# A recurrence and a SwiGLU block on one core: the transposed k made by VectorE and DRAM, the state's matmuls put beside the following unit's scores, sums merged, the beginning in another order

## The chip, the cores and the metric

The kernel runs on one core of a Trainium2 chip. The metric is the time of one execution on the device in microseconds (us), as the median of several runs. The profile is that of one further execution, with times from the start of its span. All arithmetic is in 32-bit floats; the weights arrive as 64-bit words and are made into 32-bit floats on the chip.

## The reference

The input is `q`, `k`, `v` and `f_logit`, each 4 batches x 8 heads x 768 positions x 48, and three weight matrices. A gated linear recurrence runs over the positions of each batch and head, and its output, laid out as 3072 tokens of 384, goes through a SwiGLU block of 1536 hidden values:

```python
f = 1.0 / (1.0 + np.exp(-f_logit))
for t in range(S):
    state = f[:, :, t, :, None] * state + np.einsum('bhd,bhe->bhde', k[:, :, t], v[:, :, t])
    y[:, :, t] = np.einsum('bhd,bhde->bhe', q[:, :, t], state)
x = y.transpose(0, 2, 1, 3).reshape(B * S, H * D)
g = x @ w_gate
out = (g * (1 / (1 + np.exp(-g))) * (x @ w_val)) @ w_out
```

## The kernel before

**Units.** The 768 positions are cut into 6 chunks of 128. A unit is one batch and one chunk (all 8 heads), so there are 24, taken chunk by chunk, with b = 0 to 3 in each. `short_path` does the work; `general_path` follows only if the smallest product of gates in a chunk, which `judge` looks at near the end, is below 2^-60, and in these runs it is not.

**One unit's attention** is the generator `attention(u)` (from line 518); each `yield` ends a step, and the caller decides when the next one is traced. Keys, queries and gates are held transposed, as 48 rows of one head under 48 rows of another in each of four blocks of 128 positions. ScalarE makes the sigmoid (L532, or L535 in the first two chunks). From chunk 2 on (`SQUARES`), the input is loaded as 32x32 squares that VectorE's stream transpose turns (L538 for the gates, L545 for `kT`, L565 for `qT`); before that TensorE transposes it. A scan on VectorE (L549) gives `tails`, the products of the gates to the chunk's end; its first column, `whole`, is the decay of the whole chunk. `kT` is multiplied by it (L559), which is the decayed k. A second scan gives `head` (L562), by which `qT` is multiplied (L568). `decayed` is the state times `whole` (L572).

TensorE then makes the scores `sc` from `kT` and `qT` (L586, 8 matmuls, which are 16 records in the profile), and transposes `kT` into the bank `kt` (L590, 4 records), which ScalarE copies to SBUF (L594). VectorE multiplies the scores by the causal mask into `A` (L596, twice). The output `y` is `decayed` times `qT` plus `v` times `A`: for b < 3 in two banks with 64 columns of weights a time (L614, L618), then two copies on ScalarE and 10 small DMAs from SP's queue into `xT`; for b = 3 with 32 columns a time, from a `diagonal` form of `decayed` that ScalarE copies (L578), straight into the layout of `xT` (L639, copy L654). The state's increment `dS` is `kt` times `v` (L659, 16 records of 48 columns), and VectorE adds it to `decayed` (L666). In the last chunk `kt` and `dS` are left out.

**The feed-forward block.** Chunk 0 uses plain matmuls (`mlp_plain`: `gate` and `val` at L712, down at L737), while the weights still come in; a weight is fetched, its sizes are taken by two ScalarE operations (`sizes`) and joined by VectorE (`joins`). From chunk 1 on `mlp_fifteen` multiplies the two 384 x 384 block matrices with 15 products in place of 18 (L887), for each of four values of j. A product is two matmuls of 256 columns, four records in the profile, into one of the banks A, B and o; ScalarE copies most of them to SBUF (L892, into `c11`, `c12`, `c22`, `c31`, `c32` or `aside`), VectorE adds and subtracts them (L786, L789), ScalarE takes the silu (L903) and VectorE multiplies gate by value (L837) into the hidden tiles `h`. The 15 products of one j are called a triple here. The token sums `xs` (L847 to L862) and the hidden sums `hs` (L978 to L981) are VectorE's. The down matmul, `down_seven`, uses 7 products in place of 8 (L990, and L1054 for the last, `seven`), whose results VectorE adds into `ob`. Its outputs leave by DMA from ScalarE's queue (`put_out`, L999).

**The order.** The attention of chunk c + 1 is woven into the feed-forward block of chunk c. From chunk 1 on the order is written out by hand: a counter `now` grows by `PRODUCT` (0.86) for a product and by half of `DOWN` (3.9) for half of a down product, and a step of a unit is traced when `now` passes its time in the list:

```python
    STEPS = (-2.6, -1.3, 0, 1.3, 2.8, 3.5)
    UNITS_2 = [[at + t for t in STEPS] + [*rest] for at, rest in (
        (2.6, (4, 9, 12, 14, 17.3, 17.3, 19)), (12.5, (18.2, 24, 28, 30, 34.5, 34.5, 36)),
        (28.5, (35, 41, 51.4, 52.5, 57, 57, 58)), (52, (57.1, 64, 68, 70, 72.5, 72.5, 74)))]
```

The six times from `STEPS` are those of the sigmoid and the VectorE steps up to `kT`, the seven that follow those of `head`, the transpose of q, `qT`, `sc`, `A`, `y` with `dS`, and the state. `lag` puts a VectorE operation one piece later than the product that it uses. `in_order` (L684, called at L1157 and L1219) then holds TensorE, VectorE and ScalarE to the traced order from the first unit to the middle of chunk 0's block, and again from chunk 1's block on; SP's queue is not among the three. Between the two calls `take_turns` alternates the pieces and a scheduler orders them.

**The beginning.** `run(b, step)` (L1106) works through chunk 0's units, whose attention has nothing beside it but fetching weights. Then come four joins of weights and the first steps of chunk 1's unit 4, up to L1157.

**The state's room.** All units share one `decayed` (L374). The four hidden rows of a unit are six tiles `h[j]` (L702), so each sum on them is made six times with 256 columns.

## Time and profile before

| | |
|---|---|
| median of 7 runs | 620.75 us (620.26 to 622.13) |
| profiled execution, its own time | 620.9 us |
| its span | 619.2 us |
| busy: TensorE, VectorE, ScalarE | 599.9, 500.3, 293.7 us |
| chunk 0's units alone | 0 to 31.3 us |
| chunk 0's block, with chunk 1's attention | 31.3 to 149.3 us |
| blocks of chunks 1, 2, 3, 4, with the attention of the next chunk | 94.6, 97.0, 97.1, 93.5 us |
| block of chunk 5, alone, down to its last half product | 76.7 us |
| last half product and last stores | 11.0 us |
| VectorE: stream transpose of 128x512 (L545) | 1123 ns |
| VectorE: sum of 128x256 on hidden tiles (L789) | 421 ns |
| ScalarE: copy of `kt`, 128x512 (L594) | 586 ns |
| ScalarE: table load | 1283 ns |
| store of one output tile, 192 KB, issue to landing | 2.0 us |
| loads of 96 KB squares, issue to landing | 2.3 to 2.4 us |

In the profile a row of a group has the line, the engine, the operation and its operands, the number of instructions, the total busy time, the mean in ns of one, and after the second bar the idle time of the engine just before them with what ended it. In a row in order of time the first number is the start, the second the length, and square brackets hold the idle time before it and its releaser. PE is TensorE's matmuls, PEld its weight loads, DVE VectorE, ACT ScalarE, POOL GpSimd; SPq and ACTq are DMA issues in the queues of SP and ScalarE. A matmul's length overlaps that of the next, so lengths of TensorE rows are not additive; starts are.

### The profile page before, as it was taken

The numbers are of one execution on the slowest core, as the hardware profiler recorded it, in microseconds if no ns is written. First come the engines' busy times: TensorE is split into PE (matmuls) and PEld (weight loads), VectorE is DVE, ScalarE is ACT, GpSimd is POOL, SyncE is SP. The second block draws the span as 40 slices with busy tenths as digits, with TensorE's granted clock in tenths as the row PEclk, the third lists the DMA queues.
The fourth block names the chain that finished last, engine by engine and source line by source line (L and its number), as shares of the span: only waits on it lengthen the run. The fifth ranks groups of instructions, "written<-read, shape, count | busy, mean of one in ns | idle before, by whom it ended". The sixth has DMA issues, their size and how long they took to land.

```text
span 619.2 us, 10913 instructions
## 1 busy us (share of the span) xinstructions
PE 599.9 (97%) x4060; PEld 489.5 (79%) x4060; DVE 500.3 (81%) x961; ACT 293.7 (47%) x535; POOL 5.0 (1%) x27
## 2 busy tenths in 40 slices
PE   7898999999999999999999999999999999999995
PEld 4744545667888898888899788899888889888895
DVE  7889999878999978868897877987887984566741
ACT  2485645313875621557711557632367641365600
POOL 1000000000000000000000000000000000000000
PEclk9999999999999999999999999999999999999998
DMA  9999573005231324212224320323331300100001
GB/s 149 240 244 251 172 233 90 5 23 160 63 87 49 79 69 125 67 47 65 52 72 121 91 52 19 83 62 95 110 77 29 79 7 9 51 2 0 1 2 56
DMA packets 95678, 50.95 MB, mean 82 GB/s; under 512 B 56064, under 2 KB 89472, under 8 KB 95616
## 3 DMA queue, kind: packets, MB, share of 16 engines
q1 hardware_dynamic: 92304, 45.64, 30.4%
q10 hardware_dynamic: 3312, 4.52, 2.0%
q8 instruction: 34, 0.56, 0.4%
q14 instruction: 28, 0.23, 0.1%
HBM read 42.47 MB, written 4.72 MB: 76 GB/s over the span
## 4 chain that ended last, share of the span: by engine, by line
PE 81%; DVE 9%; ACT 4%; DMA 3%; issue 2%; SPq 1%; ACTq 0%; DVEq 0%
PE o L990 16%; PE A L887 16%; PE B L887 13%; PE o L887 5%; PE c L887 5%; PE o L737 5%; PE sc L586 4%; PE val L712 4%; PE gate L712 3%; PE y L618 2%; PE kt L590 2%; PE y L614 1%; PE dS L659 1%; DVE head L562 1%; DMA ksquares<-in_k_dram 1%
## 5 line engine op out<-in xcount | busy, mean ns | idle before, releaser
L887 PE MATMUL A<-xs,w_both 128*128 128x256 f32 x240 | 62.5, 383 | 3.5 <-ACT c L892 2.3
L990 PE MATMUL o<-w_out,h 128*128 128x192 f32 x360 | 62.1, 327 | 0.2 <-ACT aside L892 0.2
L990 PEld LDWEIGHTS o<-w_out,h 128*128 128x128 f32 x360 | 58.6, 190 | 0.8 <-ACT aside L892 0.4
L887 PEld LDWEIGHTS A<-xs,w_both 128*128 128x128 f32 x240 | 44.5, 190 | 12.5 <-ACT c L892 3.9
L892 ACT COPY c<-A 128x512 f32<-128x512 f32 x40 | 23.4, 584 | 64.9 <-DVE ob L786 33.9
L786 DVE TENSOR_TENSOR c<-c,aside 128x512 f32<-128x512 f32 x60 | 41.1, 686 | 14.8 <-ACT aside L892 13.8
L892 ACT COPY aside<-A 128x512 f32<-128x512 f32 x60 | 35.0, 583 | 32.8 <-PE A L887 32.8
L789 DVE TENSOR_TENSOR c<-c,aside 128x512 f32<-128x512 f32 x60 | 41.2, 687 | 7.3 <-ACT aside L892 7.3
L837 DVE TENSOR_TENSOR h<-h,c 128x256 f32<-128x256 f32 x100 | 41.4, 422 | 7.0 <-ACT h L903 6.7
L990 PE MATMUL o<-ws,h 128*128 128x192 f32 x240 | 41.7, 328 | 0.0
L887 PE MATMUL B<-xT,extra 128*128 128x256 f32 x160 | 41.4, 381 | 0.0
L887 PE MATMUL c<-xT,w_both 128*128 128x256 f32 x160 | 41.3, 380 | 0.0
L887 PE MATMUL A<-xs,extra 128*128 128x256 f32 x160 | 41.2, 380 | 0.0
L887 PE MATMUL B<-xs,w_both 128*128 128x256 f32 x160 | 41.1, 379 | 0.0
L903 ACT ACTIVATE h<-c 128x256 f32<-128x256 f32 x100 | 39.2, 415 | 3.2 <-DVE c L789 2.0
L892 ACT COPY aside<-B 128x512 f32<-128x512 f32 x60 | 35.0, 583 | 10.7 <-PE B L887 10.1
L990 PEld LDWEIGHTS o<-ws,h 128*128 128x128 f32 x240 | 39.2, 190 | 0.3 <-issue 0.2
L789 DVE TENSOR_TENSOR c<-o,c 128x512 f32<-128x512 f32 x40 | 27.6, 689 | 14.7 <-ACT h L903 9.5
L596 DVE TENSOR_TENSOR A<-sc,causal 128x512 f32<-128x512 f32 x48 | 30.6, 678 | 6.0 <-PE sc L586 6.0
L887 PEld LDWEIGHTS B<-xs,w_both 128*128 128x128 f32 x160 | 30.4, 190 | 4.1
L887 PEld LDWEIGHTS c<-xT,w_both 128*128 128x128 f32 x160 | 30.2, 190 | 4.4 <-DVE c L789 0.2
L887 PEld LDWEIGHTS A<-xs,extra 128*128 128x128 f32 x160 | 30.3, 190 | 4.2
(134 smaller groups left out, 1154.6 us busy)
## 6 DMA issues: line engine op xcount, KB each, us to landing
fsquares<-in_f_logit_dram SPq DMA_DIRECT2D x64, 96.0 KB, 2.3
ksquares<-in_k_dram SPq DMA_DIRECT2D x64, 96.0 KB, 2.3
qsquares<-in_q_dram SPq DMA_DIRECT2D x64, 96.0 KB, 2.4
v<-in_v_dram SPq DMA_DIRECT2D x24, 192.0 KB, 3.1
w<-in_moe_w_gate_dram SPq DMA_DIRECT2D x6, 768.0 KB, 6.2
w<-in_moe_w_val_dram SPq DMA_DIRECT2D x6, 768.0 KB, 5.4
w<-in_moe_w_out_dram SPq DMA_DIRECT2D x6, 768.0 KB, 5.7
out_dram<-ob ACTq DMA_DIRECT2D x23, 192.0 KB, 2.0
```

The costliest lines, as they stand in the source:

```text
L586: nc.tensor.matmul(sc[par][:, a * C:(a + 1) * C], lhsT=kT[r, a, :], rhs=qT[r, a, :], start=True, stop=True)
L590: nc.tensor.transpose(p[:, a * C:(a + 1) * C], kT[:, a, :], ident)
L596: nc.vector.tensor_tensor(A[:, par], sc[par].rearrange("p (a t) -> p a t", t=C), causal.unsqueeze(1).broadcast_to((128, HP, C)), ALU.mult)
L712: nc.tensor.matmul(p, lhsT=w[:, j, i, :], rhs=xT[c][:, i, :], start=(i == 0), stop=(i == KT - 1))
L737: nc.tensor.matmul(p, lhsT=h[n // 2][:, n % 2 * 2 + b // 2, b % 2 * C:(b % 2 + 1) * C], rhs=w_out[:, j, :], start=(n == 0), stop=(n == NF ...
L786: nc.vector.tensor_tensor(dst, a, b, ALU.add)
L789: nc.vector.tensor_tensor(dst, a, b, ALU.subtract)
L837: lagging.append(lambda: f(*args))
L887: nc.tensor.matmul(p[name][:, n, :], lhsT=weights_of[a][:, n, j, :], rhs=tokens[b], start=fresh and n == 0, stop=True, skip_group_check=True)
L892: nc.scalar.copy(t, p[name])
L903: nc.scalar.activation(dst, src[:, 0, :], AF.Silu)
L990: nc.tensor.matmul(p[:, n, :], lhsT=lhsTs[j][:, n * C:(n + 1) * C], rhs=rhs[:, j, :], start=first and j == order[0] and n == 0, stop=j == ...
```

## The change

The parts, in the order of the diff:

- The decayed k in transposed form. For chunks 2 to 4 TensorE no longer transposes `kT`. VectorE's stream transpose turns each 32x32 square into `beside` (in the buffer of `head`), four DMAs from SP's queue write it to a tile `turn` in DRAM in rows of 32 values, and one DMA reads it back as `kt`. Chunks 0 and 1 keep the matmul transposes.
- Loads of the next unit's squares are issued singly, each right after its room is free, and `v`'s after `dS`.
- Two `decayed` tiles are used in turn.
- `dS` of a unit and the state's sum are given the time of the following unit's `sc` (just before it) and of its `A`, where they were given that of the unit's own `y`. The times in the list change: `SCORES` holds the times of `sc`, `BEHIND` those of `A` and `y` after it. From chunk 3 on the third unit starts at 22.9 where it was 28.5.
- The hidden tiles of even and of odd j are one tile each, and the sums on them are made three at a time (768 columns). Two token sums become one of 512 columns.
- The halves of `seven` get a bank each, and their outputs leave from SP's queue.
- The beginning: one join and two `sizes` come earlier, unit 4's sigmoid is made on the raw input (`sigmoid_ahead`), so that after the transpose there is only a copy, the loads of unit 5 come later and together. SP joins the engines that `in_order` holds.

```diff
+    def sigmoid_ahead(u):
+        fr = raw["f"][u % NRAW]
+        nc.scalar.activation(fr, fr, AF.Sigmoid)
+        ahead.add(u)
...
+        flat_decayed = two_decayed[u % len(two_decayed)]
+        decayed = flat_decayed[:, 0:HP * D].rearrange("p (a d) -> p a d", d=D)
...
-            nc.scalar.activation(pairs(gate)[:, :, 1:N1], p, AF.Sigmoid)
+            nc.scalar.activation(pairs(gate)[:, :, 1:N1], p, AF.Copy if u in ahead else AF.Sigmoid)
...
+        if SQUARES <= c < NCH - 1:
+            beside = att.tile([128, n], FP32, tag="head", name="beside", bufs=1)[:, 0:HP * C]
+            beside = beside.rearrange("p (i m) -> p i m", i=NI)
+            nc.vector.transpose(beside.rearrange("p i (a e) -> p a i e", e=Q), kT.rearrange("p a (i e) -> p a i e", e=Q))
+            turn = turn_pool.tile([Q, NI, HP, NI, Q], FP32, tag="turn", name="turn")
+            for r in range(NI):
+                nc.sync.dma_start(out=turn[:, :, :, r, :].rearrange("t i a e -> t (i a) e"),
+                                  in_=beside[Q * r:Q * (r + 1)].rearrange("t i (a e) -> t (i a) e", e=Q))
         yield
...
-        if c < NCH - 1:
+        if c < SQUARES:
             p = bank("kt")
             for a in range(HP):
                 nc.tensor.transpose(p[:, a * C:(a + 1) * C], kT[:, a, :], ident)
         yield
-        if c < NCH - 1:
-            kt = att.tile([128, H, W], FP32, tag="kt", name="kt")
-            nc.scalar.copy(kt, p.rearrange("t (h d) -> t h d", d=W))
+        kt = att.tile([128, HP * C], FP32, tag="kt", name="kt")
+        if c < SQUARES:
+            nc.scalar.copy(kt, p)
+        elif c < NCH - 1:
+            nc.sync.dma_start(out=kt, in_=turn.rearrange("t i a r e -> i t (a r e)"))
...
+        load_v_after(u)
         yield
...
+    def load_v_after(u):
+        if units[u][1] >= SQUARES and u + 2 < len(units):
+            load(u + 2, "v")
...
-    def hidden_tile():
-        return ffn.tile([128, 4, TH], FP32, tag="h", name="h", bufs=NP)
+    def hidden_tile(h, j):
+        if j % 2 not in h:
+            h[j % 2] = ffn.tile([128, NP // 2, 4, TH], FP32, tag="h", name="h", bufs=2)
+        return h[j % 2][:, j // 2]
...
-    UNITS_2 = [[at + t for t in STEPS] + [*rest] for at, rest in (
-        (2.6, (4, 9, 12, 14, 17.3, 17.3, 19)), (12.5, (18.2, 24, 28, 30, 34.5, 34.5, 36)),
-        (28.5, (35, 41, 51.4, 52.5, 57, 57, 58)), (52, (57.1, 64, 68, 70, 72.5, 72.5, 74)))]
-    UNITS = [[at + t for t in STEPS] + [*rest] for at, rest in (
-        (-10, (-6, 1, 6, 8, 10.5, 10.5, 12)), (6.5, (12, 18, 22.5, 24.5, 27, 27, 29)))] + UNITS_2[2:]
+    SCORES = [[12, 28, 51.4, 68], [6, 22.5, 51.4, 68]]
+    UNITS = [[[k + t for t in STEPS] + [*rest] for k, rest in zip(ks, rests)] for ks, rests in (
+        ((2.6, 12.5, 28.5, 52), ((4, 9, 9.1), (18.4, 24, 24.1), (35.6, 41, 41.1), (57.1, 64, 64.1))),
+        ((-10, 6.5, 22.9, 52), ((-6, 1, 1.1), (12.3, 18, 18.1), (30.1, 37, 37.1), (57.1, 64, 64.1))))]
+    BEHIND = ((2, 6.2), (2, 7.5), (1.1, 5.6), (2, 4.5))
+    for n, at in enumerate(SCORES):
+        following = at[1:] + [whole + SCORES[1][0]]
+        for b in range(B):
+            UNITS[n][b] += [at[b], at[b] + BEHIND[b][0], at[b] + BEHIND[b][1], following[b] - 0.01,
+                            following[b] + BEHIND[(b + 1) % B][0] - 0.01]
...
-                for j in order:
-                    lag(minus, h[j][:, 0, :], s1[j], h[j][:, 0, :])
+                for odd in range(2):
+                    lag(minus, h[odd][:, :, 0, :], s1[odd], h[odd][:, :, 0, :])
...
         def seven(n):
-            if n == 0:
-                kept["p"] = bank2("o3", "A")
+            p = bank2("o3", "Ao"[n])[:, n, :]
...
-            lag(put_out, 0, n, nc.sync if n and c == NCH - 1 else nc.scalar)
+            lag(put_out, 0, n, nc.sync)
...
         run(b - 1, 4)
+    joins.pop(0)()
+    sizes.pop(0)()
     run(B - 1, 3)
+    sizes.pop(0)()
     joins.pop(0)()
     run(B - 1, 4)
 
     hidden, last = mlp_plain(0)
     steps = attention_steps(1)
-    for _ in range(2):
-        sizes.pop(0)()
-        joins.pop(0)()
-    load(B + 1, "v")
+    sigmoid_ahead(B)
+    joins.pop(0)()
     for _ in range(2):
         sizes.pop(0)()
     hidden[0]()
@@
     hidden[1]()
     weights()
+    load(B + 1)
     hidden[2]()
     steps.pop(0)()
-    in_order(mark, (mybir.EngineType.PE, mybir.EngineType.DVE, mybir.EngineType.Activation))
+    in_order(mark, (mybir.EngineType.PE, mybir.EngineType.DVE, mybir.EngineType.Activation, mybir.EngineType.SP))
```

In chunk 1 the parts of a unit in `attention_steps` become 3, 5, 3, 3 where they were 3, 5, 2, 3; there the step with `beside` is empty, so this only counts the added `yield`.

## The prediction

> **What bounds the kernel now.** I read the page's busy shares and its 40 slices first, then busy times by stage, then TensorE's instructions in order of time, then the waits.
>
> ```profile
> PE 599.9 (97%) x4060; PEld 489.5 (79%) x4060; DVE 500.3 (81%) x961; ACT 293.7 (47%) x535; POOL 5.0 (1%) x27
> ...
> PE   7898999999999999999999999999999999999995
> ```
>
> The program is one long TensorE stream. Only the first 50 us and the last ten have visible holes. By stage (length, then busy time of PE, PEld, DVE, ACT and POOL, the granted clock, the DMA share, GB/s):
>
> ```profile
> 149.30:243.90 94.60, 94.14 (x698) 83.29 (x697) 87.62 (x164) 50.65 (x95) 0.42 (x1) 1.00 0.33 83
> 243.90:340.90 97.00, 96.13 (x706) 84.89 (x705) 80.42 (x159) 48.97 (x93) 0.42 (x1) 1.00 0.28 73
> 340.90:438.00 97.10, 96.23 (x706) 85.18 (x706) 80.66 (x160) 48.80 (x93) 0.42 (x1) 1.00 0.28 73
> 438.00:531.50 93.50, 92.44 (x625) 80.97 (x625) 73.06 (x145) 44.84 (x87) 0.42 (x1) 1.00 0.17 46
> ```
>
> The last row is the window in which chunk 5's units run, which need no `kt` and no `dS`; TensorE is idle 1 us or less in each. So a TensorE instruction removed here is time removed, less what the order loses. TensorE in order of time, with a `kt` (chunk 4) and without (chunk 5):
>
> ```profile
> 304.52 1.13 PE L887 MATMUL A<-xT,w_both 128*128 128x256 f32 x4
> 305.58 1.16 PE L586 MATMUL sc<-qT,kT 48*128 48x128 f32 x16
> 306.67 0.66 PE L590 MATMUL kt<-idf,kT 128*128 128x128 f32 x4
> 307.16 4.07 PE L990 MATMUL o<-w_out,h 128*128 128x192 f32 x24
> ...
> 444.80 1.16 PE L586 MATMUL sc<-qT,kT 48*128 48x128 f32 x16
> 445.89 1.13 PE L887 MATMUL B<-xs,extra 128*128 128x256 f32 x4
> ```
>
> Durations overlap, so I take start to start: `sc` 1.09 us, `kt` 0.49. A product (four records) takes 0.86; straight after `sc` it takes 0.97, after `kt` 0.86.
>
> The stall that returns at every chunk's start:
>
> ```profile
> 339.21 4.33 ACTq L999 DMA_DIRECT2D out_dram<-ob  x2
> ...
> 343.59 0.59 ACT L892 COPY c<-A 128x512 f32<-128x512 f32 x1 [8.63 <-DVE ob L786]
> ...
> 344.23 1.13 PE L887 MATMUL A<-xs,w_both 128*128 128x256 f32 x4 [0.58 <-ACT c L892]
> ```
>
> ScalarE's queue holds the output of `seven`, which waits for VectorE's `ob`. The copy of the first product, which frees bank A for the fourth, stands behind it. The third product starts at 342.62, the fourth at 344.23: 1.61 us instead of 0.86, and the fourth itself 0.97.
>
> [...]a product lasts 0.96 before `sc` or `y`, and 0.97 after them. [...]here 128x256 takes 422 ns and 128x512 687, thus 157 ns fixed. [...]No run here shows the price of 128-byte writes to DRAM.
>
> **The change part by part.** Signs are of the time.
>
> *`kt` off TensorE, `dS` beside the next scores* (12 units, chunks 2 to 4). Before, a unit with `y` in two banks costs 0.10 into `sc`, 1.09, 0.49, 0.10 into `y`, 0.60, 0.92, `dS` 0.55, 0.11 out: 3.96. After: 0.10 into `dS`; `dS` ahead of `sc` 0.60 (15.52 to 16.13 in chunk 0, where the two already stand so); 1.09; 0.11; 0.10; 0.60; `y` ahead of a product 1.02 (chunk 5); 0.11: 3.73. So -0.23 for nine units. For the three with b = 3, whose `y` runs at 128x32 and has the same cost out either way, -0.49 + 0.11 = -0.38. Sum -3.2. Bounds: -2.0[...], -4.6 if the moved `dS` is free.
>
> *VectorE's share.* 12 transposes at 1.12 us (the row of `kT<-ksquares`) add 13.4 us. Merged sums: each chunk 24 of 0.42 become 8 of 768 columns, 157 + 768 x 1.035 = 0.95: -2.5, over five chunks -12.6; merged token sums -0.8. Net nothing, and TensorE hides it. But merging pays late in each chunk, and the transposes come early. In 155 to 205 VectorE is busy 49.9 of 50 us and two fall there: 0 to +1. I take 0, because the nearest consumer in the order, `y` of unit 8, has 1.1 us to spare and is put one product (0.86) later. ScalarE loses 12 copies of 0.59, which were not on the path.
>
> *The round trip.* Four writes of 512 pieces of 128 B and one read of 2 KB rows. `v` has 1024 pieces of 192 B and lands in 3.1 us. Twice the pieces: 4 us as my estimate[...], then some 2.5 for the read. Four things wait behind it: `dS` has at least 20 us from the transpose (decayed ends at 160.0, next `sc` at 181.0); the next unit's `head`, whose buffer the transpose borrows, has 8.5 us in one case, 9.7 in three, 12 or more elsewhere; what stands behind `kt`'s load on SP's queue (`yT` to `xT`, three to four products later); SP's issues, five more per unit. All fit: 0.
>
> *Output of `seven` to SP's queue.* The chunk-start stall goes: 0.75 + 0.11, at four starts (245.6, 342.6, 439.5, 533.2): -3.4. What is late next: the copy's own chain, 0.2 + 0.59 after the first product, is ready 0.9 us before the fourth. So all of it counts. On SP the two stores wait for `ob` with the next unit's `turn` behind them, 15 us early.
>
> *The third unit's sigmoid.* Its start moves from 25.9 to 20.3 in the list from chunk 3 on, so on ScalarE it now stands between `c31`'s copy and the silu, with both table loads. TensorE's thirteenth product waits for the `aside` copied after them: 0.2 + 0.58 + 1.28 + 0.63 + 1.28 + 0.32 + 0.58 = 4.9 us after the ninth ends. TensorE has three products and `dS` + `sc` in between: 2.6 + 1.8 = 4.4. +0.55 in three windows: +1.6 (bounds 0 and +2). The same chain with one load makes the stall that stays:
>
> ```profile
> 351.99 1.28 ACT L903 ACT_TABLE_LOAD   x1
> ...
> 354.23 0.73 PEld L887 LDWEIGHTS A<-xs,w_both 128*128 128x128 f32 x4 [0.69 <-ACT aside L892]
> ```
>
> `y` moved to a triple's end hides a 0.13 us hitch there in each of three windows: -0.4.
>
> *The beginning.*
>
> ```profile
> 51.01 0.68 DVE L568 TENSOR_TENSOR qT<-qTp,head 128x512 f32<-128x512 f32 x1
> ...
> 51.83 1.16 PE L586 MATMUL sc<-qT,kT 48*128 48x128 f32 x16 [1.83 <-DVE qT L568]
> ```
>
> TensorE runs unbroken from 31.28, then waits here, after two matmuls of `val` (1.72 us) that the changed order puts behind `sc`. So it arrives at 48.1. VectorE: the first join (1.9 us) now fills the 1.25 us it waited at 26.75, delays A by 0.7 (`gate` still starts near 31.3, since its join is done), and brings the four joins' end from 37.5 to 35.6. The early sigmoid saves ScalarE two table loads of 1.28, so the 1.6 us wait for `top` at 42.9 shrinks to some 0.6; 0.5 waits for the next weights. I get `qT` at 49.1 instead of 51.7: TensorE stalls 1.1 with 1.7 us of `val` still ahead, against 1.83 with none. -0.9. If VectorE gains nothing, +1.6; if `qT` is there in time, -2.0.
>
> *The end.* `seven`'s halves get a bank each; 612.18 shows both halves' `ob` added after the last matmul, and both DMAs (612.6, 612.9) landing together at 617.0. Now one add of 0.35 and one DMA remain; the first store of this kind landed after 2.8. From 612.5: 615.7, -1.3 (0 to -1.6).
>
> Two decayed states remove a buffer wait that nothing on TensorE showed: 0.
>
> Sum: -3.2 - 3.4 + 1.6 - 0.4 - 0.9 - 1.3 = -7.6. The profiled execution took 620.9 (span 619.2 and 1.7 around it), 0.15 over the median of 620.75. So a span of 611.6 and a median of 613.1; I say 613.0.
>
> **The rivals.**
> *VectorE or ScalarE becomes the bound.* Stages with VectorE at 100% take the transposes as delay (+1 in 149 to 208, +0.5 in two later windows), the sigmoid's chain costs 2, the beginning loses 1.6 instead of gaining 0.9. For it: VectorE busy 87.62 of 94.60 us in the first of the windows; against: TensorE's slack to `qT` is 3 to 8 us in later windows. -7.6 + 2 + 0.4 + 2.5, and less where only some come: 615.5 to 618.
> *More is gained.* `dS` moved at no cost (-1.4), no sigmoid stall (-1.6), `qT` in time (-1.1): 609.
> *The other side: the round trip is late.* `head` holds VectorE until `turn` has landed, in order, so all of VectorE stands behind it. It begins at 7.3 us of landing (8.5 less the transpose) and costs TensorE once VectorE's slack of 1 to 4 us is used up. To eat 7.6 us in 12 units, the four writes would have to land in some 13 us; six times as long as the 2.3 of a 96 KB load. At 15 us: about 625. Against: the DMA share is 0.17 to 0.33 in these windows.
> *It does nothing:* the transposes do leave the list and the store does change queues, so only cancelling sums could give this.
>
> **How the numbers follow.** As drawn up: 0.62, with its own range 610.5 to 615.5. VectorE or ScalarE takes over: 0.20. More gained: 0.12. Late round trip: 0.05. No effect: 0.01. From 609 to 617.5 leaves out the rival on the other side, and the tails of the two next to it. Faster by over 0.2% (619.5; about what seven runs of 0.3% spread can tell): 0.94; within: 0.01; slower: 0.05.
>
> **What would show it.** Right: `sc` goes straight to a product of 0.97; `dS` to `sc` 0.60; windows of 97 us shrink to about 95; no wait of A for `c` at chunk starts; a new wait for `aside` at the thirteenth product of the second triple; the last `ob` a single add. Wrong: VectorE waiting at `head` for DMA `turn`; TensorE waiting for `kt` by DMA; a longer wait of the fifth unit's `sc`.

## The result, and the profile after

The changed kernel takes 618.62 us in the median of 14 runs (616.32 to 620.51), against 621.93 for the kernel before in 35 runs, those of the prediction's table among them. The ratio is 0.9951, with a 95% interval of 0.9941 to 0.9962. So it is faster, by some 3 us, where 7.6 were forecast, and it lies above the range. The kernel before lies either at 620.0 to 621.2 or near 622, with a mean granted clock of 0.996 to 0.999 in the first group and 0.994 to 0.996 in the second where the series list it, so below ratios are compared and not medians of different series. One ratio is uncertain by 0.10 to 0.23%, that is 0.6 to 1.4 us, and a difference of two ratios by somewhat more. The profiled execution took 618.05 us, its span 616.0.

The page has TensorE at 595.6 us instead of 599.9, and VectorE as busy as it was:

```profile
PE 595.6 (97%) x4012; PEld 484.5 (79%) x4012; DVE 500.4 (81%) x888; ACT 286.6 (47%) x522; POOL 5.0 (1%) x28
```

By stage, cut at the first product of each block, the blocks of chunks 1 and 2 are (length, then busy time of PE, PEld, DVE, ACT, POOL, the granted clock, DMA share, GB/s):

```profile
147.07:243.87 96.80, 94.41 (x674) 82.83 (x672) 89.78 (x152) 49.89 (x92) 0.42 (x1) 1.00 0.42 103
243.87:339.57 95.70, 94.88 (x689) 83.36 (x689) 81.45 (x146) 47.09 (x89) 0.42 (x1) 1.00 0.39 95
```

The first of them has 2.4 us in which TensorE is idle, where the kernel before had 0.5 in the same stretch. The same cuts in both kernels, beside what the terms of the prediction's sum give for each stretch:

| stretch | before | after | change | forecast |
|---|---|---|---|---|
| to the first product of chunk 1's block | 147.48 | 147.07 | -0.4 | -0.9 |
| block of chunk 1 | 96.38 | 96.80 | +0.4 | -1.1 |
| block of chunk 2 | 97.04 | 95.70 | -1.3 | -1.5 |
| block of chunk 3 | 96.92 | 95.70 | -1.2 | -1.5 |
| block of chunk 4 | 93.67 | 94.77 | +1.1 | -0.4 |
| block of chunk 5 to the last matmul | 80.66 | 79.80 | -0.9 | -0.9 |
| last matmul to the end of the span | 7.06 | 6.16 | -0.9 | -1.3 |
| sum | | | -3.2 | -7.6 |

One `dS` (0.60) has moved from the block of chunk 1 into that of chunk 4, since each now waits for the next unit's scores; with that put right the block of chunk 1 is 1.0 us longer than before, and that of chunk 4 is 0.5 longer.

What TensorE waited for in the changed kernel, in total us, times and the longest:

```profile
PE A L929 <- ACT aside L934: 3.4, 7, 1.1
PE fTp L542 <- DMA fraw<-in_f_logit_dram: 2.8, 2, 2.4
...
PE c L929 <- ACT c L934: 2.0, 1, 2.0
```

Before, this view had 2.3 us in four waits of A for `c`, at the chunk starts, 1.3 in five for `aside` and 1.7 for `fraw`. The four waits at the chunk starts are gone. In their place there is more waiting for `aside`, one wait of 2.0 us for `c`, and one of 2.4 us for the fourth unit's `f` in the beginning. The wait of 1.8 us of chunk 1's first unit for `qT` is gone too.

**What came as forecast.** TensorE in order of time where a unit's scores stand now:

```profile
250.01 0.67 PE L690 MATMUL dS<-v,kt 128*64 128x48 f32 x16
250.61 1.16 PE L615 MATMUL sc<-qT,kT 48*128 48x128 f32 x16
251.70 1.13 PE L929 MATMUL B<-xs,extra 128*128 128x256 f32 x4
252.67 1.03 PE L929 MATMUL c<-xT,w_both 128*128 128x256 f32 x4
```

Start to start, `dS` takes 0.60, `sc` 1.09, the product behind it 0.97: the prediction's numbers. At a chunk's start (all engines, the rows between left out) the copy no longer stands behind the store, which is on SP's queue, and the fourth product starts at 342.16, 0.86 after the third:

```profile
340.63 0.59 ACT L934 COPY c<-A 128x512 f32<-128x512 f32 x1 [6.39 <-PE A L929]
...
341.76 0.85 SPq L1037 DMA_DIRECT2D out_dram<-ob  x2
...
342.16 1.03 PE L929 MATMUL A<-xs,w_both 128*128 128x256 f32 x4
```

At the end one add follows the last matmul (the first row), where there were two (the second row, of the kernel before):

```profile
609.87 0.35 DVE L830 TENSOR_TENSOR ob<-c,o 128x192 f32<-128x192 f32 x1 [1.59 <-PE o L1091]
...
612.18 0.62 DVE L786 TENSOR_TENSOR ob<-c,o 128x192 f32<-128x192 f32 x2 [2.29 <-PE o L1054]
```

**What did not: the first window.** All engines around the 2 us wait, rows between left out:

```profile
189.34 0.42 DVE L881 TENSOR_TENSOR h<-h,c 128x256 f32<-128x256 f32 x1
...
189.85 0.59 ACT L934 COPY c<-c 128x512 f32<-128x512 f32 x1 [3.30 <-DVE h L881]
...
190.49 1.13 PE L929 MATMUL c<-xT,w_both 128*128 128x256 f32 x4 [1.98 <-ACT c L934]
```

The twelfth product of the third triple needs bank c, whose copy on ScalarE needs the room that VectorE's multiplication `h` at 189.34 sets free, and that multiplication stands in a VectorE queue that has next to no gap from 157 to 207 us (busy 49.83 of the 50 us; before, 49.76). The 5 us around the wait, in the changed kernel and then in the one before (TensorE's busy time comes first, VectorE's is the third):

```profile
187.00:192.00 5.00, 3.02 (x28) 2.08 (x26) 4.97 (x13) 1.50 (x4) 0.00 (x0) 1.00 0.67 157
...
187.00:192.00 5.00, 5.00 (x63) 4.16 (x62) 5.00 (x9) 2.86 (x7) 0.00 (x0) 1.00 0.08 22
```

Before, the same copy stood at 189.19 and the product at 191.67, because `y` and `dS` of the second unit came ahead of it:

```profile
189.19 0.59 ACT L892 COPY c<-c 128x512 f32<-128x512 f32 x1 [1.49 <-DVE h L837]
...
189.59 0.67 PE L614 MATMUL y<-qT,decayed 48*64 48x128 f32 x16
...
191.67 1.13 PE L887 MATMUL c<-xT,w_both 128*128 128x256 f32 x4
```

Counted from the first product of the block, the copy begins 1.07 us later than before (42.78 instead of 41.71), and TensorE is there for the product 2.75 us earlier (41.44 instead of 44.19).

**The last window.** The third unit's sigmoid, with a table load on either side, stands ahead of the `aside` that the thirteenth product needs, as forecast. In the blocks of chunks 2 and 3 the wait is 0.54 us each (the first row). In the block of chunk 4, whose units have no `dS`, TensorE is there 0.60 earlier and waits 1.14; the second of the loads and what stands behind it:

```profile
273.97 1.13 PE L929 MATMUL A<-xs,w_both 128*128 128x256 f32 x4 [0.54 <-ACT aside L934]
...
463.14 1.28 ACT L945 ACT_TABLE_LOAD   x1
...
464.75 0.57 ACT L934 COPY aside<-A 128x512 f32<-128x512 f32 x1
...
465.38 1.13 PE L929 MATMUL A<-xs,w_both 128*128 128x256 f32 x4 [1.14 <-ACT aside L934]
```

### The profile page after: what moved, and what is told of

It reads as the page before. It is cut to its first block, busy times and chain, and to the rows that moved or that the text cites. A ratio compares the mean times of both kernels' runs of the same rounds, so it can differ in the third digit from the quotient of the medians.

```text
span 616.0 us, 10805 instructions
## 1 busy us (share of the span) xinstructions
PE 595.6 (97%) x4012; PEld 484.5 (79%) x4012; DVE 500.4 (81%) x888; ACT 286.6 (47%) x522; POOL 5.0 (1%) x28
## 3 DMA queue, kind: packets, MB, share of 16 engines
q10 hardware_dynamic: 2016, 2.75, 1.3%
## 4 chain that ended last, share of the span: by engine, by line
PE 82%; DVE 6%; ACT 4%; DMA 3%; issue 1%; SPq 1%; ACTq 0%; DVEq 0%
PE o L1028 20%; PE A L929 14%; PE B L929 10%; PE gate L751 5%; PE val L751 5%; PE o L774 5%; PE o L929 4%; PE c L929 4%; PE o L1091 3%; PE sc L615 3%; PE y L649 2%; PE y L670 2%; PE dS L690 1%; PE y L645 1%; DMA fraw<-in_f_logit_dram 1%
```

## The experiments

Each is an edit of the changed kernel, unless it says otherwise. "Against the changed kernel" is the difference of the two ratios to the kernel before, times 621 us. Windows of the traces are compared where they say more than a ratio. Some profiles have stretches of 3.41 us, or two or three times that, in which the granted clock is 0.50 in place of 1.00. In one of them two products start 1.71 us apart (157.94 and 159.65, in the run with the sums on GpSimd), where 0.86 is usual, so my estimate is that each 3.41 us cost 1.7; where one fell in a window that is used, it says so. The last section tells where they stand.

### The outputs of `seven` on ScalarE's queue again

```diff
-            lag(put_out, 0, n, nc.sync)
+            lag(put_out, 0, n, nc.sync if n and c == NCH - 1 else nc.scalar)
```

> The changed kernel with the outputs of seven on ScalarE's queue again (the very last one on SP's, as before). Theory: at four chunk starts ScalarE's copy of the first product stands behind the store that waits for ob, and the fourth product waits 0.58 us for bank A and pays 0.11 for restarting: +0.86 at each, +3.4 us against the changed kernel, with the wait of A for the copy back in the trace. Rival: the stall only took the place of another wait of the same chain (ScalarE is late at the chunk's start anyway), then under +1.5 us.

Measured: ratio 1.0005 (0.9995 to 1.0015), +3.4 us. The wait is back at all four starts, with ScalarE's copy behind the first store:

```profile
342.31 0.34 ACTq L1037 DMA_DIRECT2D out_dram<-ob  x1
...
342.69 0.58 ACT L934 COPY c<-A 128x512 f32<-128x512 f32 x1 [7.96 <-DMA qsquares<-in_q_dram]
```

The fourth product waits 0.51 us for that copy, at 343.32. By the trace the blocks of chunks 2, 3 and 4 are 0.76 to 0.78 us longer each. The theory holds, and with it this term of the sum: without it the changed kernel is no faster than the one before.

### What a `kt` on TensorE costs (an edit of the kernel before)

```diff
-            for a in range(HP):
-                nc.tensor.transpose(p[:, a * C:(a + 1) * C], kT[:, a, :], ident)
+            for _ in range(2 if c >= SQUARES else 1):
+                for a in range(HP):
+                    nc.tensor.transpose(p[:, a * C:(a + 1) * C], kT[:, a, :], ident)
```

> The kernel before with the four transposes of kT made twice over (into the same bank) in the 12 units of chunks 2 to 4. Theory: TensorE is the path and a kt costs what stands between its start and the next, 0.49 us: +5.9 us, so that taking kt away must have gained 4.6 (0.11 a unit come back[...] behind sc). Rival: part of kt's time is cover for waits that come right after (ScalarE's copies, A for y): then clearly less, under +4 us.

Measured: ratio 1.0093 (1.0075 to 1.0111), +5.8 us, so 0.48 us a unit. By the trace the blocks of chunks 1 to 3 are 1.75 us longer each, 0.44 a unit. Little or nothing of a `kt`'s 0.49 us is cover.

### The third unit's sigmoid at its old time, without and with the second unit's `y`

```diff
-        ((-10, 6.5, 22.9, 52), ((-6, 1, 1.1), (12.3, 18, 18.1), (30.1, 37, 37.1), (57.1, 64, 64.1))))]
+        ((-10, 6.5, 28.5, 52), ((-6, 1, 1.1), (12.3, 18, 18.1), (35.6, 41, 41.1), (57.1, 64, 64.1))))]
```

> The changed kernel with the third unit of chunks 3 to 5 started at 28.5 again instead of 22.9 (its head and transpose of q at 35.6 and 41). Theory: the waits of 0.54, 0.54 and 1.14 us for aside at the thirteenth product of the second triple come from the sigmoid with its two table loads in front of that copy; they go: -2.2 us, -2.5 with the restarts, against the changed kernel. Rival: the pair of loads costs the same where it goes to, in the third triple or behind it; then within 0.5 us of the changed kernel and a new wait for aside or c elsewhere.

Measured: ratio 0.9954 (0.9938 to 0.9970), +0.2 us. The three waits for `aside` are gone, and three of 0.50 for `c` stand seven products later, for a copy that stands between the same pair of loads, behind the first and the sigmoid:

```profile
277.17 1.28 ACT L547 ACT_TABLE_LOAD   x1
...
279.00 0.57 ACT L934 COPY c<-B 128x512 f32<-128x512 f32 x1
...
279.62 1.13 PE L929 MATMUL B<-xT,extra 128*128 128x256 f32 x4 [0.50 <-ACT c L934]
```

The rival was right. In the kernel before the same place had shown no wait; there `y` and `dS` of the second unit stood over it:

```profile
278.59 1.28 ACT L532 ACT_TABLE_LOAD   x1
...
278.75 0.67 PE L614 MATMUL y<-qT,decayed 48*64 48x128 f32 x16
```

The next edit adds this to the late sigmoid:

```diff
-            UNITS[n][b] += [at[b], at[b] + BEHIND[b][0], at[b] + BEHIND[b][1], following[b] - 0.01,
+            UNITS[n][b] += [at[b], at[b] + BEHIND[b][0], at[b] + (4.5 if n and b == 1 else BEHIND[b][1]), following[b] - 0.01,
```

> The changed kernel with the third unit of chunks 3 to 5 started at 28.5 again, as in the run with the late sigmoid, and besides the second unit's y three products earlier (27 in the list instead of 30, where it stood before the change). Theory: the table loads at 25.9 were hidden before the change because the second unit's y and dS stood over them; with y back there the 0.50 us waits for c go, and the 0.54, 0.54 and 1.14 us waits for aside are not there either: -1.5 to -2.2 us against the changed kernel. Rival: the pair of loads, 3.2 us of ScalarE, finds a wait wherever it stands: within 0.5.

Measured: ratio 0.9925 (0.9906 to 0.9945), -1.6 us. The blocks of chunks 2, 3 and 4 are 95.10, 95.10 and 93.55 us, together 2.4 less than in the changed kernel, with `y` over the pair:

```profile
468.13 1.28 ACT L547 ACT_TABLE_LOAD   x1
468.29 0.67 PE L645 MATMUL y<-qT,decayed 48*64 48x128 f32 x16
```

So the sigmoid's move and `y`'s move cost 2.4 us between them. Undoing the sigmoid's move alone gained nothing; undoing `y`'s alone was not tried.

### The wait in the first window: order or VectorE's total

Five edits bear on it. First, `y` of the second unit ahead of the waiting product, as it was:

```diff
+    Y_EARLIER = 0.9
...
-            UNITS[n][b] += [at[b], at[b] + BEHIND[b][0], at[b] + BEHIND[b][1], following[b] - 0.01,
+            UNITS[n][b] += [at[b], at[b] + BEHIND[b][0], at[b] + BEHIND[b][1] - (Y_EARLIER if n == 0 and b == 1 else 0), following[b] - 0.01,
```

> The changed kernel with the y of the second unit of chunk 2 one product earlier (list time 34.6 instead of 35.5), so that it stands ahead of the product that waits 1.98 us for bank c. Theory: what the change moved is TensorE's cover: before, y (1.52 us) and dS (0.55) stood ahead of that product, now neither does; with y back the wait falls to some 0.5 us, -1.5 us against the changed kernel. Rival: VectorE, never idle from 157 to 207 us, sets the pace of the whole stretch, and the 1.5 us appear as a wait at a later product: within 0.5 us of the changed kernel.

Measured: ratio 0.9945 (0.9926 to 0.9964), -0.4 us, and the block of chunk 1 is 96.62 instead of 96.80. The wait falls from 1.98 to 0.38, but waits of 0.39 for `aside` and 0.27 for `c` and smaller delays follow, and by 205 us TensorE has given back all but 0.3 us of the gain. The rival was right: order moves the wait, it does not remove it.

Second, three of the sums of the down weights later:

```diff
-    DOWN_SUMS_AT = (22, 24, 26, 42)
+    DOWN_SUMS_AT = (36, 38, 40, 42)
```

> The changed kernel with the first three sums of the down weights (1.37 us each on VectorE) at 36, 38 and 40 in the list instead of 22, 24 and 26. Theory A, VectorE's backlog: the 1.98 us wait of TensorE for bank c at 190.5 us comes from VectorE, which is never idle from 157 to 207 us; with 4.1 us of sums put behind that point the copy of c is 4 us earlier, the wait goes, -2.0 us against the changed kernel. Theory B: the sums have to be made anyway and VectorE stays full until 207 us, so the wait comes back some products later: 0 to -0.5 us, or worse if the down product then waits for its sums.

Measured: ratio 0.9986 (0.9977 to 0.9996), +2.2 us. The wait near 190 is gone, and one of 2.65 us for VectorE's `c` stands at 204.46, still in the full stretch:

```profile
204.46 1.84 PE L929 MATMUL c<-xT,w_both 128*128 128x256 f32 x4 [2.65 <-DVE c L833]
```

The profile has 3.41 us at half the clock right behind it; without the 1.7 us estimated for these, the block is 0.7 longer than in the changed kernel. The ratio says more than that, and the rest is not explained. So theory A is out: the three sums are still inside the full stretch, and the wait comes back some products later, as theory B has it.

Third, VectorE's new transposes twice over:

```diff
-            nc.vector.transpose(beside.rearrange("p i (a e) -> p a i e", e=Q), kT.rearrange("p a (i e) -> p a i e", e=Q))
+            for _ in range(2):
+                nc.vector.transpose(beside.rearrange("p i (a e) -> p a i e", e=Q), kT.rearrange("p a (i e) -> p a i e", e=Q))
```

> The changed kernel with VectorE's transpose of the decayed k made twice over in all 12 units (0.70 us more each). Theory: VectorE is the bound of the first window only, where it is never idle from 157 to 207 us; three of the 12 transposes fall there (at 159.5, 180.3 and 200.6), so they cost 3 x 0.70 = +2.1 us, as more waiting of TensorE near 190 and 204 us, and the other nine, in windows where VectorE has idle time within some us, cost nothing or 0.3 together: +1.6 to +2.4. Rival 1: the wait near 190 us comes from the order on TensorE alone and VectorE has slack: within 0.5. Rival 2: VectorE bounds all windows: +5 or more.

Measured: ratio 0.9997 (0.9983 to 1.0010), +2.9 us. The blocks of chunks 2, 3 and 4 have the lengths of the changed kernel to 0.01 us: eight doubled transposes cost nothing there. The block of chunk 1 is 99.80, of which by the same estimate 1.7 are 3.41 us at half the clock, so +1.3, and the wait near 190 grows from 1.98 to 2.87:

```profile
192.90 1.13 PE L930 MATMUL c<-xT,w_both 128*128 128x256 f32 x4 [2.87 <-ACT c L935]
```

Rival 2 is out, and rival 1 too. In the block the size is below the forecast of 2.1, by the ratio above it; which of the three transposes found slack is not shown.

Fourth, the sums on GpSimd:

```diff
+        def minus(dst, a, b):
+            nc.gpsimd.tensor_tensor(dst, a, b, ALU.subtract)
...
-    DOWN_SUMS_AT = (22, 24, 26, 42)
+    DOWN_SUMS_AT = (4, 4.1, 4.2, 4.3)
```

> The changed kernel with the four sums of the down weights made by GpSimd, which does nothing else then, instead of VectorE (four times 1.37 us in the first window). Theory: VectorE is the bound from 157 to 207 us, so with 4.1 us of its work gone ahead of 190 us the 1.98 us wait goes: -2 us against the changed kernel. Rival: [...]VectorE's operations beside it last longer by about what it is spared: within 0.7, with 512-column sums clearly longer than 0.69 us.

Measured: ratio 1.0070 (1.0056 to 1.0084), +7.4 us, for a reason beside the question. GpSimd's order is not held, so it began the sums at 136.5, ahead of the block, and held VectorE up there:

```profile
139.71 5.71 POOL L869 TENSOR_TENSOR ws<-w_out,ws 128x1152 f32<-128x1152 f32 x2
139.84 3.10 DVE L830 TENSOR_TENSOR extra<-extra,w_both 128x512 f32<-128x512 f32 x1
```

A 512-column sum of VectorE's took 3.10 us beside a sum on GpSimd, and 0.68 at 150.19, when GpSimd was done; one of 256 columns took 2.84 at 137.08 and 0.42 at 151.85. What makes them so long is not shown. TensorE waited 2.8 and 4.5 us at the block's start, and from 151.3 to 161.5 us its granted clock was 0.50. With the sums out of VectorE's queue there was no wait near 190 us, which speaks for VectorE's total, but in a block so disturbed it is weak evidence. The fifth edit is the clean one:

```diff
-    DOWN_SUMS_AT = (22, 24, 26, 42)
+    DOWN_SUMS_AT = (22, 24, 62, 42)
```

> The changed kernel with one sum of the down weights (1.37 us on VectorE, at 26 in the list) moved to 62, behind the stretch in which VectorE is never idle; nothing needs it before the product called five, at 71. Theory: VectorE's total in 157 to 207 us sets that stretch, so 1.37 us less of it is 1.2 to 1.4 us less of TensorE's waiting near 190 us, -1.3 us against the changed kernel, with nothing given back. Rival: as with all three sums moved, the wait comes back near 204 us: 0, or slower.

Measured: ratio 0.9942 (0.9927 to 0.9957), -0.6 us, within the noise of the ratio; but the block of chunk 1 is 95.52 instead of 96.80, so 1.37 us less of VectorE's work is 1.28 us less there, and nothing comes back behind it. (The block is 96.79 to 96.87 in three other profiles that leave it as it is, those of the outputs of `seven` and of the late sigmoid with and without `y`; it is 95.51 again in the kernel with all edits together, below.) What is left of the wait:

```profile
189.06 1.13 PE L929 MATMUL c<-xT,w_both 128*128 128x256 f32 x4 [0.70 <-ACT c L934]
```

VectorE's total in the stretch from 157 to 207 us sets that stretch: work taken out of it shortens the block by nearly as much (1.28 for 1.37), work added lengthens it (1.3 for three transposes of 0.70), and work moved inside it, on VectorE or on TensorE, does not shorten it by more than 0.2 us. It was full before as well, and TensorE did not wait there.

### The beginning

```diff
+        if u == 1:
+            load(3, "f")
+            fetches.pop(0)()
         if u + NRAW < B:
-            load(u + NRAW, "fkq")
+            load(u + NRAW, "fkq" if u == 0 else "kq")
         load(u + 1, "v")
-        fetches.pop(0)()
+        if u:
+            fetches.pop(0)()
```

> The changed kernel with the load of the fourth unit's f issued ahead of the first fetch of weights (768 KB) instead of behind it. Theory: TensorE's wait of 1.95 to 2.36 us for fraw near 20.5 us, which four of five profiles of the new beginning show and the kernel before has with 0.80, goes; some of it is given back at the waits for qT and for the weights: -0.8 to -1.3 us at the end. Rival: the weights, then some 1.5 us later, hold up the first join or the sizes, and the start of gate stays where it is: 0.

Measured: ratio 0.9942 (0.9927 to 0.9957), -0.6 us, not told apart from nothing. The wait for `fraw` is gone, and `gate` begins at 30.61. But the scores of chunk 1's first unit wait 1.19 us for `qT` instead, and chunk 1's block begins at 146.99 instead of 147.07. In the changed kernel the same three places are:

```profile
20.81 0.63 PE L542 MATMUL fTp<-idf,fraw 128*128 128x128 f32 x4 [2.36 <-DMA fraw<-in_f_logit_dram]
...
32.37 2.84 PE L751 MATMUL gate<-xT,w_both 128*128 128x512 f32 x6
...
49.53 1.16 PE L615 MATMUL sc<-qT,kT 48*128 48x128 f32 x16
```

The second edit is the whole old beginning: `load_ahead` and the lines from `run` to `in_order` as they were.

> The changed kernel with the whole beginning up to the first stretch of plain feed-forward as it was before (joins, sizes, the sigmoid behind the transpose, loads, SP's queue free). Theory of the prediction: the new beginning is worth 0.9 us, so +0.9. Rival from the profile: the wait for qT (1.83 us) is gone, but 1.1 us were lost ahead of 32 us to fraw, so +0.4, or nothing.

Measured: ratio 0.9973 (0.9962 to 0.9984), +1.4 us; by the trace +0.8 at the first product of chunk 1's block. So the new beginning is worth about what was forecast. One profile tells little of it: in the profiles of this same beginning that have the full clock in it, chunk 1's block begins anywhere from 145.1 to 147.1, with a wait of 2.0 to 2.4 us for `fraw` in some and none in others. What makes the load arrive late in one execution and not in the next stays open.

### An earlier table load, and all together

On top of the late sigmoid with the earlier `y`, a silu of eight zeros loads the table ahead of the copy:

```diff
+    nothing = const.tile([128, 8], FP32, tag="nothing", name="nothing")
+    nc.gpsimd.memset(nothing, 0.0)
...
+    waiting += [(n * whole + 6.0, lambda: nc.scalar.activation(nothing, nothing, AF.Silu)) for n in (1, 2, 3)]
```

> The kernel with the late sigmoid and the earlier y, and a silu of eight zeros on ScalarE at 6.0 in the list of the blocks of chunks 2 to 4, so that the table is loaded ahead of the ninth product's copy, where ScalarE has a hole of 2.17 us. Theory: the wait of 0.29 us for aside (0.40 with the restart) at the thirteenth product of the first triple goes in three windows: -1.2 us against the same kernel without it, 3.5 to 4 against the changed kernel. Rival: the load delays another copy: no difference.

Measured: ratio 0.9878 (0.9857 to 0.9899), -4.5 us against the changed kernel. The blocks of chunks 2 to 4 are 94.54, 94.54 and 93.00, each 0.55 shorter than without it, a little more than the 0.40 forecast; the load stands in the hole over `sc`:

```profile
250.31 1.16 PE L617 MATMUL sc<-qT,kT 48*128 48x128 f32 x16
250.42 1.28 ACT L1237 ACT_TABLE_LOAD   x1
```

Then this, the third sum at 62 and the fourth `f` ahead of the weights in one kernel:

> The changed kernel with the late sigmoid and the earlier y, the early table load, the third down sum at 62, and the fourth f ahead of the weights. Theory: the gains lie in different places and add: -2.3, -1.2, -1.3 and -0.6 make -5.4 us against the changed kernel. Rival: they overlap: under -4.

Measured: 611.10 us, ratio 0.9842 (0.9827 to 0.9857), -6.8 us. The blocks of chunks 1 to 4 are 95.51, 94.54, 94.54 and 93.00: together they are 5.4 us shorter than in the changed kernel, as forecast: the gains add, as they lie in different places.

### `dS` at its own unit's `y`, and the round trip

```diff
-            UNITS[n][b] += [at[b], at[b] + BEHIND[b][0], at[b] + BEHIND[b][1], following[b] - 0.01,
-                            following[b] + BEHIND[(b + 1) % B][0] - 0.01]
+            y = at[b] + BEHIND[b][1]
+            UNITS[n][b] += [at[b], at[b] + BEHIND[b][0], y, y, y + 1.7]
```

and the read of `kt` moved up, ahead of `sc`.

> The changed kernel with dS and the state's sum back at the unit's own y (chunks 2 to 4), and the read of kt issued ahead of the unit's scores instead of behind them, so that it can be there. Theory: kt off TensorE is what gains (0.49 less 0.11 for each of 12 units, -4.6 us), and putting dS ahead of the next scores costs some 0.16 a unit[...], +1.9 us; so this kernel is 1.5 to 2.5 us faster than the changed one, the wait of 1.98 us in the first window falls by up to 0.5 with it. Rival: the round trip through DRAM (writes landing some 4.2 us after the transpose begins, then the read) is too late for the unit's own y, and dS waits for kt in most units: over 1 us slower than the changed one, with TensorE waiting for a DMA ahead of dS.

Measured: ratio 1.0187 (1.0164 to 1.0209), +14.7 us. The rival was right: TensorE waits for `kt` 15.8 us in 11 waits. The read alone takes 6.3 us:

```profile
239.35 0.59 SPq L612 DMA_DIRECT2D kt<-turn  x1
...
245.63 0.67 PE L690 MATMUL dS<-v,kt 128*64 128x48 f32 x16 [1.24 <-DMA kt<-turn]
```

Then, on top of this, the read in four parts:

```diff
-            nc.sync.dma_start(out=kt, in_=turn.rearrange("t i a r e -> i t (a r e)"))
+            for i in range(NI):
+                nc.sync.dma_start(out=kt[Q * i:Q * (i + 1)], in_=turn[:, i].rearrange("t a r e -> t (a r e)"))
```

> The kernel with dS at the unit's own y, in which TensorE waited for kt 15.8 us in all, with the read of kt from DRAM cut into four DMAs of 32 rows instead of one of 128. The one read took 6.3 us from issue to use, with 128 packets of 124 ns spread over 4.4 us, as if some four engines carried it. [...]kt lands 3 to 4 us after the first issue, and the waits for kt go: -12 us or more against that kernel, and within 2 us of the changed one. Rival: the read is slow for what it reads (rows just written), then four reads take as long, and the waits stay.

Measured: ratio 0.9979 (0.9968 to 0.9990), 13 us faster than the run before it and 1.7 slower than the changed kernel. Each part lands 1.9 to 3.0 us after its issue, 2.0 in the median, the last of the four 3.2 to 4.4 us after the first issue, for an estimate of 3 to 4, and no `dS` waits for a DMA any more:

```profile
233.26 1.71 SPq L613 DMA_DIRECT2D kt<-turn  x4
...
237.75 0.67 PE L691 MATMUL dS<-v,kt 128*64 128x48 f32 x16
```

The same bytes from the same place, so the memory is not what was slow. The packets of the two traces differ as the times do. During one read of 128 rows at most 6 or 7 of its 2 KB packets are under way at once, 3.4 to 4.1 in the mean of a read (at most 6, and 3.4 to 3.9, in the 12 reads of the changed kernel); during four reads it is up to 17, and 4.6 to 8.2 in the mean. And each of the 12 single reads leaves 5 updates of its semaphore in the trace, each of the 48 short reads 16. What decides how many packets are under way at once is not shown; a single read of another shape was not tried. The waits for `aside` in the later windows are 1.14 us in all three without `dS` ahead of `sc`, where two were 0.54; that is at least a part of why this kernel is still slower than the changed one.

> All the edits together (late sigmoid, earlier y, early table load, third down sum at 62, f ahead of the weights), and dS at the unit's own y with kt in four reads. Theory: dS behind y saves [...]some 0.16 us for each of 12 units, and gives cover of 0.55 us back at the wait near 188 us: -1.5 to -2.5 us against the kernel with all together. Rival: dS ahead of the next scores stood over ScalarE's table loads in later windows; without it the waits for aside come back: 0 or slower.

Measured: 609.86 us, ratio 0.9831 (0.9819 to 0.9844), the fastest of all. Against the kernel with all together it is 0.7 us by the ratio, whose intervals overlap, and 0.4 by the sum of the four blocks. The place of `dS` is worth little, less than I had read from the trace; waits of 0.19 us at three more down products take back part of what it saves.

## Why the prediction was wrong

The direction was right and the mechanism of most terms too; the sum was too large by 4.4 us in the profile. The step that failed is the one on VectorE's share: it took nothing for the stretch in which VectorE was already full, and TensorE waits 1.98 us there. The measured median lies just above the time of the first rival (VectorE or ScalarE becomes the bound, 615.5 to 618); as the ratio times the table's 620.75 it is 617.7, inside it. Of that rival's terms two came, VectorE's delay in the first window and a chain of the sigmoid of 2.2 us, and two did not: delays in the later windows, and a loss in the beginning. By the steps of the prediction:

- *VectorE's share*: wrong, by 2.0 us. The prediction had the evidence in hand (VectorE busy 49.9 of 50 us in 155 to 205; its own windows add up to 49.8), bounded the step at 0 to +1, and took 0 "because the nearest consumer in the order, `y` of unit 8, has 1.1 us to spare". But `y` was not the nearest consumer. The product that waits 1.98 us reuses a bank and waits for the bank's copy on ScalarE, that copy (3.30 us of idle time before it) waits for VectorE's multiplication, and this product stood behind the very `y` and `dS` that the change moves. In a stretch that VectorE sets, what TensorE is spared gains nothing either, which the sum did not allow for: the block is 1.0 us longer than before, about as much as the copy is later (1.07). The step also balanced VectorE's total over the program, though the transposes come in the full stretch and the merged sums save behind it, as the step itself said. The total came out right (500.3 before, 500.4 after) in part by luck, as two prices were off and mostly cancelled. The transposes, priced at 1.12 us by the row of another one, took 0.70, so 8.4 us and not 13.4. The hidden sums saved 9.2 us of busy time (46.5 before, 37.3 after) and not 12.6: one of 768 columns took the 0.95 us forecast from VectorE's sums of 256 and 512 columns (422 and 687 ns), but the 120 small ones had overlapped in part, with lengths that add up to 50.3. The run with one sum less in the stretch shows that VectorE's total there counts nearly one for one.
- *The third unit's sigmoid*: right in mechanism and, in two windows, to 0.01 us. In the third it was 1.14 instead of 0.55: the `dS` that was counted as cover does not exist in chunk 5. What the step missed is that `y`, moved at the same time, had covered the old place.
- *`kt` off TensorE, `dS` beside the next scores*, and `y` at a triple's end: forecast -3.6 together; what is left of the four blocks when the two waits above and `seven` are taken out is -2.7. The 0.10 and 0.11 put beside `sc`, `y` and `dS` are read from starts (a product of 0.96 before them and 0.97 behind, where it is 0.86 otherwise); their cause is not shown. The price of `kt` is confirmed to about a tenth (0.44 to 0.48 for 0.49); where the rest went was not shown.
- *Output of `seven`*: right, -3.4 forecast, and 3.4 lost when it was undone (0.77 a block by the trace, 0.86 forecast).
- *The beginning*: -0.9 forecast, -0.4 in the profile and some -1.4 by the run that undid it. The size is right, but in this profile not for the reasons given: the stall for `qT` did not shrink from 1.83 to 1.1, it went, because `gate` began at 32.37 and not near 31.3, after a wait of 2.36 us for `fraw` that the sum did not have. Where that wait was taken away, the stall was 1.19, as forecast.
- *The end*: -1.3 forecast, -0.9 measured; the one add is there as forecast.
- *The round trip*: "All fit: 0" was right, and the four writes, put at 4 us, landed within 4.2 of the first issue where each was timed. But the read was put at 2.5 us and took 6.3 where it was timed; it fits only because `dS` was moved by a unit.

So -7.6 became -3.2 by +2.0 (VectorE), +0.6 (sigmoid in the last window), +0.9 (`kt`, `dS`, `y`, which is what remains when the others are taken out), +0.5 (beginning, in this profile) and +0.4 (end).

## What to carry to other kernels

Where an engine off the path is busy in every slice of a stretch, look at each bank or buffer that is reused there and follow it to that engine, and count its work by stretch and not over the program: here 1.37 us taken from a full stretch gained 1.28, and eight transposes added in blocks that were not full cost nothing. When an instruction is moved on the bounding engine, ask what it stood over as well as what it costs: `y` and `dS` had hidden a table load and a late copy, which without them showed as waits of 0.50 us at three places and of 1.98 at one. And ask what stands behind a DMA in the queue of a computing engine: here the store in ScalarE's queue held back a copy at four chunk starts, and undoing its move to SP's queue lost 3.4 us.

## What the runs showed that was not expected

A read of 256 KB from DRAM took 6.3 us to its use as one DMA of 128 rows, with at most 6 or 7 packets under way at once, and landed after at most 4.4 us as four DMAs of 32 rows, with up to 17; why is not shown. Writes of 128-byte pieces took no longer than the loads: 64 KB in 512 pieces landed 2.2 us after issue in the median, where 96 KB loads took 2.2 to 3.0. The stream transpose of 128x512 took 1.1 us into `gates`, `kT` and `qT`, and 0.70 us into `beside`; this too is not explained.

And the granted clock was 0.50 for short stretches. Apart from the first microseconds, of which there is no record, and the very end, the 18 profiles have 13 stretches with a granted clock of 0.50, eleven of 3.41 us, one of 6.83 and one of 10.24; 3.41 us at half the clock cost 1.7 by the estimate above, about half of what this change gained. Some stand close behind a wait of TensorE. In the run with three sums later, the product behind the wait of 2.65 us lasted 1.84 us, where it lasts 1.13 behind the wait of 1.98 in the changed kernel. In the run with `f` ahead of the weights, TensorE waited 2.02 us until 190.45, and the clock was 0.50 from 191.22 to 194.63 (0.83 in the mean of this window):

```profile
190.00:200.00 10.00, 9.55 (x60) 7.47 (x61) 9.96 (x17) 5.18 (x12) 0.00 (x0) 0.83 0.14 39
```

The wait alone is not enough for it: the changed kernel's own profile has waits of 2.36 and 1.98 us and the full clock behind both. No run tested what decides.
